# Sixteen attention steps ahead of two MLP layers: one of two heads normalised on ACT, bias tables on GpSimd, one triangle on DVE, and sixty more fill products

## The chip, the core and the metric

The kernel runs on one core of one Trainium2 chip. The core has five engines with queues of their own: TensorE (PE), ScalarE (ACT), VectorE (DVE), GpSimd (POOL) and SyncE (SP), which issues most transfers. The metric is device time in microseconds; less is better. The median of three runs before the change was 915.99 us (913.09 to 917.13).

## What is computed

Attention with a causal window of 128 positions and a linear bias per head, over four sequences of 576 positions with eight heads of 64, then two MLP layers of width 2048 on the 2304 tokens of width 512. The inputs are float32.

```python
def _attn_ref(q, k, v):
    ...
    scores = scale * np.matmul(q, k.transpose(0, 1, 3, 2))
    ...
    bias = slopes[:, None, None] * (-np.abs(rel).astype(np.float32))[None, :, :]
    mask = (rel >= 0) & (rel < window)
    scores = np.where(mask, scores + bias[None], -1000000000.0)
    scores = scores - np.max(scores, axis=-1, keepdims=True)
    attn = np.exp(scores)
    attn = attn / (np.sum(attn, axis=-1, keepdims=True) + 1e-09)
    return np.matmul(attn, v)
...
    h = np.maximum(x @ w_in, 0.0)
    return h * h @ w_out
...
    h = x @ w_in
    g = h * np.cos(h)
    return g @ w_out
```

## The kernel before

Attention is cut into 72 steps. A step is one block of 128 positions (`j`) and one pair of heads: step `a` has `j = a // 4` and heads `2 * (a % 4)` and the next. Blocks whose window lies wholly in the block before and their own are of the kind plain; first, straddle and after are the kinds at the borders of a sequence (`kind`, line 318), and each kind has its own bias table of 128 columns per head in `bias_sb`. `make_bias(0)` makes the tables of the kinds first and plain, `make_bias(1)` those of straddle and after; step 16 (`j` = 4) is the first of the kind straddle.

The first sixteen steps (`START`, line 57) run before any MLP work, two at a time: eight pairs, which are counted from 0 here, pair `k` being steps `2k` and `2k + 1`. For a pair, in this order:

- `scores` (358): TensorE, in float32, into two PSUM banks that pairs use in turn.
- `minima` (403): DVE merges the columns of the block before into those above the diagonal (line 413, not for pairs 0 and 1), then adds the bias and takes the row's extreme, one operation and one read of the accumulator for each of two steps and two heads (line 424).
- `exps` (435): ACT, four exponentials with row sums (line 440).
- `normalise` (449): POOL adds a small number to the four sums (451), DVE takes the reciprocals (452) and multiplies each of the four 128x128 blocks by its own (456).
- `transposes` (458): TensorE turns the four blocks round, ACT copies them out of PSUM (466), and two selects on POOL split them into the part of the own block and that of the block before (469).
- `values` (496): TensorE multiplies with `v`, when the four steps of a block are ready (`values_of_block`). `x_hi` (ACT, 532) and `x_lo` (DVE, 535) then write the two float32r halves of the MLP's input.

Between them stand stages of weight tiles: `w_top` (ACT, 201), `w_rest` (DVE, 205), `w_split` (ACT, 217) and its low part (DVE, 220), with a POOL memset (199). They advance by one stage with each `tick`; new ones start in pairs 3 and 7 only (`START_W`).

The loop at line 739 writes the order out: in round `k` the minima of pair `k + 1`, the exponentials of pair `k`, the values of a block in odd rounds from 3 on, the transposes of pair `k - 1`, the scores of pair `k + 2`, the normalisation of pair `k`. `tc.manual_schedule(engines=ENGINES)` keeps PE, ACT and DVE in that written order; POOL and SP are ordered by a scheduler, and so is everything behind the first MLP unit. Each engine takes its queue strictly in order. After round 7 follow the transposes of pair 7, the values of block 3, and `h_mms(0)` (546), the first hidden unit of the first layer, with its relu on ACT (570). `fill` (112) issues products of a constant bfloat16 tile with itself that nobody reads; 34 of them stand before and between the first scores.

Of the kernel before, what the change touches and what calls it, by code (L numbers as in the profile page):

```python
# [10 lines left out]
BF16 = mybir.dt.bfloat16  # L11
# [4 lines left out]
ALU = mybir.AluOpType  # L16
# [37 lines left out]

START, PLAIN, FILLS = 16, 7, (19, 5, 10)


A_OPEN, START_W = 20, (3, 7)  # L60
# [19 lines left out]
def attention_mlp_mlp(ctx: ExitStack, tc: tile.TileContext, kq, s0, v, w1, w2, bias, ident, out):  # L80
# [262 lines left out]
        k = 512 * (hp // 2) + 256 * what + 128 * (hp % 2)  # L343
        return S0[j][:, k : k + 128]

    def make_bias(part):
        w = slice(256 * part, 256 * part + 256)
        for h in range(H):
            dve.tensor_scalar(bias_sb[:, h, w], base_sb[:, w], 2.0**-h, None, ALU.mult)

    def scores_to(a):
        while now["qk"] < min(a, STEPS - 1):
# [96 lines left out]
    def normalise(*steps):  # L449
        st = St.pop(steps)  # L450
        (pool if len(steps) == 2 else dve).tensor_scalar(st[:, 2], st[:, 1], 1e-9, None, ALU.add)
        dve.reciprocal(st[:, 3], st[:, 2])
        for i, a in enumerate(steps):
            for e in range(2):
                p = Pt[steps][:, 1, i, e]
                dve.tensor_scalar(p, p, st[:, 3, i, e : e + 1], None, ALU.mult)

    def transposes(*steps):

        n = len(steps)  # L460
        pt = Pt.pop(steps)
        tb = ps_s.tile([P, n, 2, P], F32, tag="s", name=f"t_{steps[0]}")
        for i in range(n):
            for e in range(2):
                te.transpose(tb[:, i, e], pt[:, 1, i, e], id_sb)  # L465
        act.copy(pt[:, 0], tb)  # L466
        if kind(steps[0] // 4) != "first":
            for part, sign in ((1, 1), (0, -1)):
                pool.affine_select(  # L469
                    pt[:, part],  # L470
                    pt[:, 0],
                    pattern=[[0, n], [0, 2], [-sign, P]],
                    compare_op=ALU.is_gt if part else ALU.is_ge,
                    fill=0.0,
                    base=0,
                    channel_multiplier=sign,
                )
        for i, a in enumerate(steps):
            Tt[a] = pt[:, :, i]
            waiting.append(a)  # L480

    waiting = []

    def values_of_block():
# [206 lines left out]
    with ExitStack():  # L691
# [12 lines left out]
            above, above, pattern=[[0, 2], [1, P]], compare_op=ALU.is_gt, fill=0.0, base=0, channel_multiplier=-1  # L704
        )
        above = above.bitcast(I32)
        id_sb = kp.tile([P, P], F32, name="id_sb")
        KS = kp.tile([P, 2, H, P], F32R, name="KS")
        base_sb = rp.tile([P, 1024], BF16, tag="a", name="base_sb")
        load_plain(0, slice(0, 1))  # L710
        act.dma_start(base_sb[:, 0:256], bias[:, 0:256])
        make_bias(0)
        load_plain(0, slice(1, 2))
        act.dma_start(id_sb, ident)
        load_plain(1)
# [13 lines left out]


        with tc.manual_schedule(engines=ENGINES):
            pairs = [(s, s + 1) for s in range(0, START, 2)]
            fill(FILLS[0])
            scores(pairs[0])
            fill(FILLS[1])
# [3 lines left out]
            for k in range(len(pairs)):  # L739
                j = k // 2 - 1  # L740
                if k + 1 < len(pairs):
                    minima(pairs[k + 1])
                if k == 0:
                    make_bias(1)
                exps(pairs[k])
                if k % 2 and j >= 0:
                    values_of_block()
                    x_hi(j)
                if k:
                    transposes(*pairs[k - 1])  # L750
                if k + 2 < len(pairs):
                    scores(pairs[k + 2])
                if k + 1 == len(pairs):
                    scores((START,))
                    minima((START,))
                normalise(*pairs[k])
                if k % 2 and j >= 0:
                    x_lo(j)
                tick("aw" if k in START_W else "a")
            transposes(*pairs[-1])  # L760
            for a in pairs[-2]:
                values(a)
            tick("a")
            for k in range(2):
                hps = slice(2 * k, 2 * k + 2)
# [131 lines left out]
```

## Time and profile before

| | |
|---|---|
| median of three runs | 915.99 us (913.09 to 917.13) |
| profiled execution, time | 915.2 us |
| profiled execution, span | 913.5 us |
| mean granted TensorE clock | 0.996 of full speed |
| TensorE busy | 897.2 us, 98% |
| DVE busy | 583.5 us, 64% |
| ACT busy | 470.8 us, 52% |
| POOL busy | 93.6 us, 10% |

Busy shares are means over the whole span. The span is the time from the first to the last instruction; 1.7 us lie around it. The part that the change touches is the first 45 us. A timeline shows instructions in order of time with what ended the wait ahead of them; a chain follows the end back, at each step to what released it; windows give the busy time of each engine in a stretch.

### The profile page before, as it was taken

What the parts mean: (1) busy time and instruction counts of PE and PEld (TensorE: products, weight loads), DVE (VectorE), ACT (ScalarE), POOL (GpSimd) and SP (SyncE); (2) the same over time, 40 slices, a digit from 0 to 9 for tenths busy, and PEclk for the clock granted to TensorE, in tenths of its full rate; (3) what the DMA queues carried; (4) which work ended last, traced back from release to release, by engine and by line L of the source; (5) the groups of instructions that cost most, each with busy time, mean ns of one, the idle gap of its engine ahead of it and who ended that gap; (6) DMA issues with size and microseconds to landing.
All of it is one profiled execution on the core that took longest, in us unless ns stands there. A gap on an engine that the chain in (4) does not pass through costs nothing.

```text
span 913.5 us, 12979 instructions
## 1 busy us (share of the span) xinstructions
PE 897.2 (98%) x4850; PEld 745.6 (82%) x4850; DVE 583.5 (64%) x1351; ACT 470.8 (52%) x1009; POOL 93.6 (10%) x163
## 2 busy tenths in 40 slices
PE   8799999999999999999999999999999999999998
PEld 6577778888888888888888888888888888888897
DVE  7799676666676666745455786665566555655553
ACT  6599554454455444545454774454444444444443
POOL 2333212101111111201011000000000000000000
PEclk9899999999999999999999999999999999999999
DMA  8762131221122111232422530020001000100010
GB/s 343 268 250 58 59 127 59 93 64 64 41 76 81 47 58 47 82 138 93 170 107 98 199 142 1 3 90 1 1 1 47 0 1 1 47 0 1 1 47 24
DMA packets 25870, 69.18 MB, mean 76 GB/s; under 512 B 2640, under 2 KB 8144, under 8 KB 25808
## 3 DMA queue, kind: packets, MB, share of 16 engines
q1 hardware_dynamic: 25376, 68.16, 21.2%
q8 instruction: 38, 0.62, 0.3%
q10 hardware_dynamic: 432, 0.20, 0.1%
q14 instruction: 24, 0.20, 0.1%
HBM read 58.91 MB, written 9.44 MB: 75 GB/s over the span
## 4 chain that ended last, share of the span: by engine, by line
PE 87%; DVE 6%; ACT 4%; issue 1%; DMA 1%; POOL 0%; DVEq 0%; ACTq 0%; POOLq 0%
PE h L564 14%; PE h L565 13%; PE h L566 13%; PE y L641 13%; PE y L643 12%; PE y L642 12%; PE o L512 3%; PE s L374 2%; PE t L465 1%; PE s L394 1%; ACT p L440 1%; PE y L631 1%; PE y L632 1%; PE y L633 1%; DVE s L424 1%
## 5 line engine op out<-in xcount | busy, mean ns | idle before, releaser
L564 PE MATMUL h<-xh,w 128*128 128x512 f32 (+1 forms) x640 | 237.9, 372 | 0.7 <-ACT a L570 0.7
L565 PE MATMUL h<-xl,w 128*128 128x512 f32 (+1 forms) x640 | 236.3, 369 | 0.0
L566 PE MATMUL h<-xh,w 128*128 128x512 f32 (+1 forms) x640 | 236.1, 369 | 0.0
L564 PEld LDWEIGHTS h<-xh,w 128*128 128x128 f32 x640 | 121.0, 189 | 22.1 <-ACT a L570 1.1
L566 PEld LDWEIGHTS h<-xh,w 128*128 128x128 f32 x640 | 120.8, 189 | 20.5
L565 PEld LDWEIGHTS h<-xl,w 128*128 128x128 f32 x640 | 121.1, 189 | 18.9
L641 PE MATMUL y<-rh,w 128*128 128x512 f32 (+1 forms) x320 | 123.4, 385 | 0.5 <-DVE ysb L656 0.5
L643 PE MATMUL y<-rh,w 128*128 128x512 f32 (+1 forms) x320 | 118.5, 370 | 0.0
L642 PE MATMUL y<-rl,w 128*128 128x512 f32 (+1 forms) x320 | 118.4, 370 | 0.0
L594 ACT ACTIVATE r<-r 128x512 f32<-128x512 f32 x72 | 45.5, 632 | 120.3 <-DVE r L593 120.3
L641 PE MATMUL y<-gh,w 128*128 128x512 f32 x256 | 99.6, 390 | 0.2 <-ACT gh L604 0.2
L642 PE MATMUL y<-gl,w 128*128 128x512 f32 x256 | 99.6, 389 | 0.0
L643 PE MATMUL y<-gh,w 128*128 128x512 f32 x256 | 99.6, 389 | 0.0
L605 DVE TENSOR_TENSOR gl<-r,gh 128x512 fp32r<-128x512 f32 x72 | 49.8, 691 | 75.5 <-ACT gh L604 75.5
L591 DVE SCALAR_TENSOR_TENSOR r<-kk,h 128x512 f32<-128x512 int32 x72 | 49.4, 686 | 62.7 <-ACT kk L590 62.6
L581 DVE TENSOR_TENSOR a<-a 128x512 f32<-128x512 f32 x62 | 44.2, 714 | 59.1 <-ACT rh L580 56.3
L590 ACT ACTIVATE kk<-h 128x512 int32<-128x512 f32 x72 | 42.9, 596 | 68.4 <-PE h L566 68.3
L570 ACT ACTIVATE a<-h 128x512 f32<-128x512 f32 x72 | 43.0, 597 | 67.8 <-PE h L566 66.4
L469 POOL TENSOR_SCALAR_AFFINE_SELECT p<-p 128x256 f32<-128x256 f32 x104 | 51.2, 493 | 249.4 <-ACT p L466 245.9
L440 ACT ACTIVATE p<-s,st 128x128 f32<-128x128 f32 x112 | 40.1, 363 | 67.7 <-DVE st L424 63.3
L643 PEld LDWEIGHTS y<-rh,w 128*128 128x128 f32 x320 | 60.3, 188 | 10.6
L641 PEld LDWEIGHTS y<-rh,w 128*128 128x128 f32 x320 | 60.4, 189 | 10.4 <-issue 1.7
(82 smaller groups left out, 1385.0 us busy)
## 6 DMA issues: line engine op xcount, KB each, us to landing
raw<-w_in SPq DMA_DIRECT2D x32, 1023.8 KB, 6.6
raw_a<-kq_in SPq DMA_DIRECT2D x44, 256.0 KB, 2.5
v<-v_in SPq DMA_DIRECT2D x18, 256.0 KB, 2.6
y<-ysb SPq DMA_DIRECT2D x18, 256.0 KB, 2.0
raw_a<-y SPq DMA_DIRECT2D x18, 256.0 KB, 2.7
out<-ysb SPq DMA_DIRECT2D x16, 256.0 KB, 2.4
s<-s_in SPq DMA_DIRECT2D x6, 512.0 KB, 9.4
s<-s_in SPq DMA_DIRECT2D x2, 256.0 KB, 3.6
```

Of the source, the lines that this page charges most:

```text
L440: act.activation(Pt[steps][:, 1, i, e], Sc[a][e][:, own(j)], AF.Exp, bias=st[:, 0, i, e : e + 1], scale=-1.0, accum_out=st[:, 1, i, e : e ...
L469: pool.affine_select(pt[:, part], pt[:, 0], pattern=[[0, n], [0, 2], [-sign, P]], compare_op=ALU.is_gt if part else ALU.is_ge, fill=0.0, b ...
L564: te.matmul(o, wh[:, cs], xh, start=(c == 0 and kt == 0), stop=False, skip_group_check=True)
L565: te.matmul(o, wh[:, cs], xl, start=False, stop=False, skip_group_check=True)
L566: te.matmul(o, wl[:, cs], xh, start=False, stop=(kt == KT - 1), skip_group_check=True)
L581: dve.tensor_tensor(a, a, a, ALU.mult)
L591: dve.scalar_tensor_tensor(r, kk, -C1, hb, ALU.mult, ALU.add)
L594: act.activation(r, r, AF.Abs)
L605: dve.tensor_tensor(rl, r, rh.bitcast(F32), ALU.subtract)
L641: te.matmul(o, wh, gh, start=(first and not (two and m % 2)), stop=False, skip_group_check=True)
L642: te.matmul(o, wh, gl, start=False, stop=False, skip_group_check=True)
L643: te.matmul(o, wl, gh, start=False, stop=last, skip_group_check=True)
```

## The change

Four things. The multiplication by the reciprocal goes to ACT for the second head of each step of a pair. The tables of the kinds straddle and after are made by POOL, behind the normalisation of pair 0. For pair 7 ACT copies the transposed blocks to the place of the part of the block before, where one select on POOL works on them in place, and DVE makes the other part by a multiplication of the PSUM tile with a constant 0/1 triangle, `onward`. And there are more fill products: four ahead of the transposes in rounds 1 to 7, four behind the scores in rounds 0 to 5, and eight between the values of pair 6 and pair 7, 60 in all.

```diff
-START, PLAIN, FILLS = 16, 7, (19, 5, 10)
+START, PLAIN, FILLS = 16, 7, (19, 5, 10, 4, 4, 8)
...
-    def make_bias(part):
+    def make_bias(part, engine):
         w = slice(256 * part, 256 * part + 256)
         for h in range(H):
-            dve.tensor_scalar(bias_sb[:, h, w], base_sb[:, w], 2.0**-h, None, ALU.mult)
+            engine.tensor_scalar(bias_sb[:, h, w], base_sb[:, w], 2.0**-h, None, ALU.mult)
...
                 p = Pt[steps][:, 1, i, e]
-                dve.tensor_scalar(p, p, st[:, 3, i, e : e + 1], None, ALU.mult)
+                r = st[:, 3, i, e : e + 1]
+                if len(steps) == 2 and e:
+                    act.activation(p, p, AF.Copy, scale=r)
+                else:
+                    dve.tensor_scalar(p, p, r, None, ALU.mult)
...
-        act.copy(pt[:, 0], tb)
+        quick = steps == pairs[-1]
+        act.copy(pt[:, 1 if quick else 0], tb)
+        if quick:
+            dve.tensor_tensor(pt[:, 0], tb, onward, ALU.mult)
         if kind(steps[0] // 4) != "first":
-            for part, sign in ((1, 1), (0, -1)):
+            for part, sign in ((1, 1), (0, -1))[: 1 if quick else 2]:
                 pool.affine_select(
                     pt[:, part],
-                    pt[:, 0],
+                    pt[:, part if quick else 0],
...
+        onward = kp.tile([P, 2, 2, P], BF16, name="onward")
+        pool.memset(onward, 1.0)
+        pool.affine_select(
+            onward,
+            onward,
+            pattern=[[0, 2], [0, 2], [1, P]],
...
-        make_bias(0)
+        make_bias(0, dve)
...
-                if k == 0:
-                    make_bias(1)
                 exps(pairs[k])
...
                 if k:
+                    fill(FILLS[3])
                     transposes(*pairs[k - 1])
                 if k + 2 < len(pairs):
                     scores(pairs[k + 2])
+                    fill(FILLS[4])
...
                 normalise(*pairs[k])
+                if k == 0:
+                    make_bias(1, pool)
...
             for a in pairs[-2]:
                 values(a)
+            fill(FILLS[5])
```

In the rows that follow, `st` tiles hold the sums and reciprocals of one pair, `s_0`, `s_1` with three figures are the banks of scores, `s_0_110` to `s_6_116` the tiles in which the exponentials of a pair stand, `t` the transposed pair in PSUM. Lines 458 and 471 of the changed kernel are the normalisation on ACT and the copy.

POOL, from the constants to the add of pair 2, before:

```order
L703 AFFINE_SELECT above<-above 128x256
L451 TENSOR_SCALAR st_224<-st_224 128x4
L451 TENSOR_SCALAR st_229<-st_229 128x4
L199 MEMSET cv_w_1_550 128x1024
L451 TENSOR_SCALAR st_264<-st_264 128x4
```

and now:

```order
L717 AFFINE_SELECT onward<-onward 128x512
L451 TENSOR_SCALAR st_227<-st_227 128x4
L349 TENSOR_SCALAR bias_sb<-base_sb 128x256 x8
L199 MEMSET cv_w_0_405 128x1024
L451 TENSOR_SCALAR st_232<-st_232 128x4
L199 MEMSET cv_w_1_605 128x1024
L451 TENSOR_SCALAR st_271<-st_271 128x4
```

The eight bias operations and the memset of the first weight tile, which stood ahead of the constants' select, now stand between the adds of pair 0 and pair 1.

ACT, from the last exponential of pair 0 to the first of pair 2, before:

```order
L440 ACTIVATE s_0_110,st_224<-s_1_198,st_224 128x128
L440 ACTIVATE s_1_111,st_229<-s_0_208,st_229 128x128
L440 ACTIVATE s_1_111,st_229<-s_1_209,st_229 128x128
L440 ACTIVATE s_1_111,st_229<-s_0_208,st_229 128x128
L440 ACTIVATE s_1_111,st_229<-s_1_209,st_229 128x128
L466 COPY s_0_110<-t_273 128x512
L440 ACTIVATE s_2_112,st_264<-s_0_246,st_264 128x128
```

and now:

```order
L440 ACTIVATE s_0_110,st_227<-s_1_201,st_227 128x128
L458 ACTIVATE s_0_110<-s_0_110,st_227 128x128 x2
L440 ACTIVATE s_1_111,st_232<-s_0_211,st_232 128x128
L440 ACTIVATE s_1_111,st_232<-s_1_212,st_232 128x128
L440 ACTIVATE s_1_111,st_232<-s_0_211,st_232 128x128
L440 ACTIVATE s_1_111,st_232<-s_1_212,st_232 128x128
L471 COPY s_0_110<-t_284 128x512
L458 ACTIVATE s_1_111<-s_1_111,st_232 128x128 x2
L440 ACTIVATE s_2_112,st_271<-s_0_241,st_271 128x128
```

The normalisations of a pair stand between its exponentials and those of the next pair, behind the copy of the pair before it.

ACT at the end of the sixteen steps, from the high half of x in round 7 to the copy of pair 7, before:

```order
L440 ACTIVATE s_0_110,st_476<-s_1_453,st_476 128x128
L532 CAST xh_106<-o_503 128x4x128
L466 COPY s_6_116<-t_523 128x512
L201 CAST cv_w_1_550<-raw_1_169 128x1024
L466 COPY s_0_110<-t_553 128x512
```

and now:

```order
L440 ACTIVATE s_0_110,st_523<-s_1_496,st_523 128x128
L540 CAST xh_106<-o_554 128x4x128
L471 COPY s_6_116<-t_578 128x512
L458 ACTIVATE s_0_110<-s_0_110,st_523 128x128 x2
L201 CAST cv_w_1_605<-raw_1_172 128x1024
L471 COPY s_0_110<-t_608 128x512
```

The cast of the second weight tile stands behind the normalisation of pair 7 and ahead of the copy that waits for its transposes.

## Rows read from the trace of the kernel before

**Rows 1.** Page: busy time, and the granted clock in 40 equal slices.

```profile
PE 897.2 (98%) x4850; PEld 745.6 (82%) x4850; DVE 583.5 (64%) x1351; ACT 470.8 (52%) x1009; POOL 93.6 (10%) x163
...
PEclk9899999999999999999999999999999999999999
```

**Rows 2.** Stretches: length, busy (instructions) of PE, PEld, DVE, ACT, POOL, granted clock, DMA.

```profile
25.00:30.00 5.00, 2.32 (x30) 1.82 (x30) 4.89 (x24) 2.66 (x11) 3.34 (x6) 1.00 1.03 402
...
20.00:40.00 20.00, 15.51 (x158) 12.58 (x160) 15.09 (x63) 11.03 (x36) 9.45 (x15) 0.88 0.72 270
40.00:60.00 20.00, 19.31 (x94) 14.54 (x91) 17.04 (x44) 18.03 (x35) 5.86 (x8) 0.95 0.79 300
60.00:80.00 20.00, 19.20 (x118) 14.52 (x117) 18.15 (x37) 19.10 (x38) 6.36 (x9) 1.00 0.23 82
```

**Rows 3.** Stretches of one microsecond around the gap of TensorE, same columns.

```profile
32.00:33.00 1.00, 0.07 (x2) 0.00 (x0) 0.90 (x7) 1.00 (x2) 0.59 (x1) 1.00 1.08 301
...
35.00:36.00 1.00, 1.00 (x9) 0.80 (x10) 1.00 (x2) 0.58 (x1) 0.20 (x1) 0.68 1.00 401
36.00:37.00 1.00, 1.00 (x12) 1.00 (x10) 0.15 (x1) 0.00 (x0) 0.93 (x2) 0.50 1.10 467
```

**Rows 4.** Chain that ended last, first 60 us: start, us, what.

```profile
8.16 1.03 DVE bias_sb L349 x8
...
12.82 0.87 DVE s L456 x4
13.70 0.67 DVE s L413 x2
...
15.51 0.87 DVE s L456 x4
...
33.24 0.60 DVE s L456
```

**Rows 5.** Timeline, 7 to 24 us: start, us, engine, line, operation [idle before].

```profile
6.96 1.27 PE L114 MATMUL junk<-idle 128*128 128x256 bf16 x10
...
8.24 0.31 POOL L451 TENSOR_SCALAR st<-st 128x4 f32<-128x4 f32 x1 [5.55 <-ACT s L440]
...
12.47 0.37 ACT L440 ACTIVATE s<-s,st 128x128 f32<-128x128 f32 x1 [0.43 <-DVE st L424]
...
14.06 0.22 POOL L451 TENSOR_SCALAR st<-st 128x4 f32<-128x4 f32 x1 [3.11 <-ACT s L440]
...
20.06 0.64 ACT L466 COPY s<-t 128x512 f32<-128x512 f32 x1
...
23.38 0.58 ACT L532 CAST xh<-o 128x512 fp32r<-128x512 f32 x1 [0.25 <-PE o L512]
```

**Rows 6.** Timeline: value products early and late, and the first relu.

```profile
15.11 1.09 PE L512 MATMUL o<-s,v 128*64 128x128 f32 x16
...
35.49 1.98 PE L512 MATMUL o<-s,v 128*64 128x128 f32 x16
...
38.55 1.97 PE L512 MATMUL o<-s,v 128*64 128x128 f32 x16
...
44.32 0.60 ACT L570 ACTIVATE a<-h 128x512 f32<-128x512 f32 x1 [0.46 <-PE h L566]
```

**Rows 7.** Durations by line, first 45 us: ns, least/median/most; starts; shapes.

```profile
L199 POOL MEMSET cv_w<- x4: 952/953/955, 1.3 to 43.2; 128x1024 f32 x4
...
L703 POOL TENSOR_SCALAR_AFFINE_SELECT above<-above x1: 407/407/407, 2.3 to 2.3; 128x256 f32<-128x256 f32 x1
...
L469 POOL TENSOR_SCALAR_AFFINE_SELECT s<-s x12: 637/637/1147, 17.7 to 36.7; 128x512 f32<-128x512 f32 x12
...
L201 ACT CAST cv_w<-raw x3: 1380/1381/1381, 17.5 to 42.5; 128x1024 f16<-128x1024 bf16 x3
...
L217 ACT CAST w<-cv_w x2: 1047/1048/1048, 24.4 to 40.8; 128x1024 fp32r<-128x1024 f32 x2
...
L220 DVE TENSOR_TENSOR w<-cv_w,w x2: 1209/1217/1225, 27.1 to 41.9; 128x1024 fp32r<-128x1024 f32 x2
```

More of the change, by code (lines that the diff above doesn't have):

```diff
@@ L480, in transposes @@
             waiting.append(a)
+    pairs = [(s, s + 1) for s in range(0, START, 2)]
     waiting = []
@@ L706, in attention_mlp_mlp @@
         above = above.bitcast(I32)
+        onward = kp.tile([P, 2, 2, P], BF16, name="onward")
[4 more added lines that the diff above has]
+            pattern=[[0, 2], [0, 2], [1, P]],
+            compare_op=ALU.is_ge,
+            fill=0.0,
+            base=0,
+            channel_multiplier=-1,
+        )
         id_sb = kp.tile([P, P], F32, name="id_sb")
@@ L731, in attention_mlp_mlp @@
         with tc.manual_schedule(engines=ENGINES):
-            pairs = [(s, s + 1) for s in range(0, START, 2)]
             fill(FILLS[0])
```

## The prediction

> **What bounds the kernel now.** I read the page's busy table first. TensorE is busy 98% of the span at a granted clock of 0.9 or more of full speed in every slice of the clock row but the second [rows 1]. The stretches of 20 us come next: from 20 to 40 us TensorE is busy 15.51 us of 20 and the clock is 0.88, in the two stretches after that it is busy over 19 us [rows 2]. All that the change touches ends at about 44 us, where the relu of the first hidden unit starts [rows 6]. So the question is by how much that relu, and the ACT work around it, comes earlier or later. Whatever it is, it runs through to the end: ACT is busy 18.03 and 19.10 us of the two stretches that follow, mostly with splitting weights [rows 2], and cannot make up lateness there; behind that TensorE sets the pace, as its 98% of the whole span says [rows 1].
>
> Next the chain that ended last, for the first 45 us. From 8 to 26 us it stays on DVE: bias tables 1.03, then for each pair the merge (0.67), four minima and four normalisations (0.87), 2.69 from one pair to the next [rows 4]. The normalisations begin at 12.82 for pair 1 and at 33.24 for pair 7 (I count pairs from 0), 20.4 us for six pairs, with two waits of the split of a weight tile and three low halves of x in between.
>
> Last, TensorE by the microsecond: it is busy 0.07 us in the microsecond from 32 to 33, while it waits for the normalisation of pair 7; from 35 to 36 the granted clock is 0.68, in the next microsecond 0.50, which is 1.2 of 2.4 GHz [rows 3]. Behind that sixteen value products take 1.97 us, earlier 1.09 [rows 6].
>
> **Bias tables on GpSimd.** DVE loses eight operations, 1.03 us of its chain [rows 4]. They go to POOL's queue, and there the order puts all eight, and a memset of a weight tile (0.95, [rows 7]) that used to run before 3 us, between the add of pair 0 and the add of pair 1. The reciprocal of pair 1 waits for that add, and behind it on DVE wait all further minima, on ACT the new normalisations. No row has a POOL tensor_scalar of 128x256 in bfloat16. Bounds: the four-element add, 0.22 [rows 5], and the select of 128x512, 0.64 without interference; nearest is the select of 128x256, 0.407 [rows 7], and I take 0.41. The add of pair 0 ends at 8.55 [rows 5]; 8.55 + 8 x 0.41 + 0.95 + 0.22 is 13.0, and with 0.3 for the reciprocal normalisation 1 starts at 13.3, 0.5 later than now. With 0.22 the queue no longer decides: DVE is ready for pair 1 at about 11.5. With 0.64 it is 15.1. Behind 16 us nobody waits for these tables: the kinds that they serve start with step 16.
>
> The Trainium skill, GPSIMD Engine Reference, section 3.1, gives 1.03 cycles of 1.2 GHz per element for operations with little work in them. As an estimate from that page, 256 elements are 0.22 us on top of what a tiny operation takes, 0.44 in all, and the sum below would end 0.2 us later. No run here shows it yet.
>
> **Half of the normalisations on ACT.** DVE loses two of four per pair, 0.43 of 0.87 [rows 4]. ACT gains two, of a form that no row has; the exponential of the same shape takes 0.37, and four of them with the reads of their accumulators, which the new operation does not have, 1.5 [rows 5]. I take 0.30, between DVE's 0.22 and 0.37. Now the order matters more than the sum. Before, ACT ran the exponentials of pair k+1 while DVE normalised pair k. In the new order ACT's two normalisations of pair k stand between the two, and they wait for POOL's add and DVE's reciprocal, which wait for the exponentials of pair k. So ACT gets a loop of its own: from the first exponential at 12.47 to the add at 14.06 are 1.6 us, the add takes 0.22 [rows 5], the reciprocal and its hand-over about 0.3, so 2.1, and the copy of a transposed pair (0.6) fits between; then two normalisations, 0.6: 2.7 us. In pairs 3, 5 and 7 the high half of x stands there too and makes it 3.1. Pairs 2 to 7: 3 x 2.7 + 3 x 3.1 = 17.4; the two weight casts on ACT, 1.38 and 1.05 long, of which some 0.1 overlaps with the next operation [rows 7], make it 19.9. That is 0.5 less than the 20.4 of now, if nothing else waits.
>
> But ACT's copy of the transposed pair, the selects and the value products now sit in this loop too. Carried forward queue by queue with the same durations, three waits come out. In pair 5 the high half of x waits for values whose selects start only after exponentials 4; copy, selects and values took 3.3 us (20.06 to 23.38), ACT gets there after 2.7, and the next copy waits for four fill products and the transposes behind the values: 1.4 together. In pair 6 the weight cast (1.05) now follows normalisation 5, DVE's subtraction (1.21) waits for it, minima 7 (1.67) wait for that, and the reciprocal comes 1.1 after ACT wants it. In pair 7 the chain copy, selects, values, fill, transposes, scores and minima of step 16 is 5.9 us against 4.6 on ACT, 1.2. Sum 3.7; I take 23.3 us for the six pairs, since part of the cast is counted in the wait of pair 6, and 36.6 for normalisation 7, 3.4 later than now; with no waits it is 33.2, as now.
>
> The Trainium skill speaks against this step: ScalarE: Activation LUTs, Rules for kernel authors, leaves multiplications to VectorE. As an estimate from its formula (section What ACT_TABLE_LOAD costs) one such operation is 386 ns, 93 of it overlapped, so 0.29 us; the row of the exponential, 367 ns, agrees to 0.02. By the rule alone ACT pays 0.6 where DVE saves 0.43, and the sum stays as it is.
>
> **The last pair and the order at the end.** One select instead of two before the value products saves 0.64; DVE's triangle runs beside ACT's copy and costs nothing, but the weight cast of 1.38 on ACT now stands between normalisation 7 and that copy, as the rows of ACT's order show, and takes some 0.6 back. The scores of step 17, which now stand ahead of the last values (these start at 38.55, [rows 6]), move partly behind them. From normalisation 7 to the relu are now 11.1 us (33.24 to 44.32). With the clock held: cast and copy to 2.5, select 0.7, second half of the values 0.7, twelve hidden products of 0.23 and their end 3.3, with the waits between them 7.5: 3.6 less. At half clock the values, the scores and the first hidden products are 2.6 longer, as they are now.
>
> **Fill products.** Sixty are added, 0.107 to 0.127 us each at full clock (ten took 1.27, [rows 5]), 7 us in all. Those behind the scores are covered by TensorE's waits for DVE or ACT. Four before the transposes cost up to 0.43 where the values came last (counted above). None stands between the scores of step 16 and the transposes of pair 7, which is where TensorE idles before the clock falls. Whether 0.43 before that gap and 0.86 behind it hold the clock is the open question. I expect that they just do, since the stretch from 25 to 30 us of now, with 2.32 busy us of 5, still had 1.00 [rows 2].
>
> **The sum.** Normalisation 7 3.4 later, the tail 3.6 shorter: 0.2 us earlier at the relu. On the profiled execution that is 915.2 - 0.2 = 915.0; the median of the three runs lies 0.8 above it, so **915.8 us**. Some later loads move in SP's queue; I cost them at nothing, as ACT stays busy over 90% from 40 to 80 us [rows 2]; if that cover failed, a load would show as a wait on ACT there.
>
> **Rivals.** *The clock falls all the same.* The gap that no fill covers is about as long as now. Then the tail is only 1.0 shorter, the net is 2.4 later, and the time 918.4. Against it: the products in front of the gap are denser.
>
> *ACT is no bound.* If the three waits vanish because the queues settle otherwise, and the bias operations take 0.22 to 0.41, normalisation 7 comes at 33.2 to 31.4, up to 1.8 earlier, and with the shorter tail the whole 3.6 to 5.4: 910.6 to 912.4. For it speaks that DVE, now the chain, loses 4.5 us; against it that the loop through ACT, POOL and DVE leaves 0.5 us at best.
>
> *POOL's queue holds up pair 1.* Place: the add of pair 1 behind eight bias operations and the memset. Each tenth of a microsecond per operation costs 0.8. From 0.44 on the kernel is slower than before with the clock held. At 0.64 it is 1.6 slower, 917.6; with the clock fallen too 4.2, 920.2. Slower by over 0.5%, 4.6 us (about what a measurement of this kernel can tell from no change), needs 1.0 per operation with the clock held or 0.7 with it fallen.
>
> **How the numbers follow.** Forecast 0.42, clock 0.26, no bound 0.22, POOL 0.10. Faster by over 0.5% is below 911.4: some two thirds of the second rival, 0.14. Slower is above 920.6: most of the last, 0.09. The rest, 0.77, is no measurable change. The range reaches from the best end of the second rival, 910.6, to 920.0; outside lie most of the last rival, 0.09, and what of the second would gain still more, 0.08.
>
> **What the profile after would show.** Right: POOL starts the add of pair 1 near 12.8; ACT waits for DVE's reciprocal before its normalisations; normalisation 7 after 35 us; the value products of pair 7 near 0.95 us and a clock of 1.00 from 30 to 45. Wrong: bias operations far from 0.41, exponentials that follow one another without those waits, a slice at 0.50, or a relu of the first unit away from 44 by more than 3 us.

## The result, and the profile after

The changed kernel is slower: 926.07 us (median of 4 runs, 925.45 to 926.26) against 915.41 of the kernel before beside it, a ratio of 1.0117 (95% interval 1.0093 to 1.0141). The prediction was 915.8, between 910.6 and 920.0. The profiled execution has a span of 924.1 us, 10.6 more than before, and the relu of the first hidden unit starts at 55.44 instead of 44.32 [rows 6], 11.1 later. So all of the loss arises in the first 55 us, as the prediction had placed it, and almost nothing of it is made up.

Page of the changed kernel: busy times, and the granted clock in 40 slices.

```profile
PE 905.9 (98%) x4910; PEld 752.5 (81%) x4910; DVE 581.1 (63%) x1328; ACT 475.5 (51%) x1025; POOL 98.9 (11%) x172
...
PEclk8999999999999999999999999999999999999999
```

Beside [rows 1] this shows nothing: the shares are the same, and a slice of 23 us is too coarse for the clock. Stretches of the same trace (columns as in [rows 2]):

```profile
10.00:15.00 5.00, 3.88 (x42) 3.04 (x38) 2.06 (x11) 2.28 (x11) 4.81 (x7) 1.00 1.03 430
15.00:20.00 5.00, 1.34 (x6) 1.01 (x7) 2.34 (x12) 2.17 (x11) 3.33 (x6) 0.70 1.00 415
20.00:25.00 5.00, 5.00 (x42) 4.04 (x42) 3.19 (x20) 2.99 (x12) 0.44 (x2) 0.62 0.83 343
...
40.00:45.00 5.00, 4.05 (x32) 3.04 (x32) 1.10 (x8) 2.65 (x11) 1.50 (x3) 0.66 0.56 197
45.00:50.00 5.00, 4.35 (x31) 3.15 (x32) 3.35 (x9) 2.73 (x5) 0.64 (x1) 0.77 0.67 280
...
60.00:80.00 20.00, 19.26 (x100) 14.59 (x99) 19.27 (x48) 19.11 (x38) 8.22 (x11) 1.00 0.58 220
```

From 10 to 15 us POOL, the engine with the least work, is busy 4.81 of 5, while DVE and ACT do 2.06 and 2.28 us of work and TensorE stops at 13.88. The granted clock falls twice: at 15 to 25 us, and again from 40 us on. From 60 to 80 us ACT is busy 19.11 of 20, about as in [rows 2], so there is no idle time in which lateness could be made up. The chain that ended last (start, us, what) says what POOL does; in [rows 4] it stood on DVE there:

```profile
7.48 1.52 ACT s L440 x8
9.07 0.23 POOL st L451
9.38 3.30 POOL bias_sb L349 x4
12.74 0.85 POOL bias_sb L349
...
16.32 0.89 POOL cv_w L199
17.29 0.24 POOL st L451
17.55 0.19 DVE st L452
17.84 0.78 DVE s L460
```

The eight table operations take 6.94 us, 0.87 from one to the next, then comes the memset, and only at 17.29 the add of pair 1. Before, it stood here:

```profile
9.63 0.31 POOL L451 TENSOR_SCALAR st<-st 128x4 f32<-128x4 f32 x1 [1.08 <-ACT s L440]
```

The timeline of the changed kernel shows who waited for it (in brackets the idle time and what ended it), and a second queue on POOL later:

```profile
17.55 0.18 DVE L452 RECIPROCAL st<-st 128x4 f32<-128x4 f32 x1 [5.50 <-POOL st L451]
...
17.83 0.69 ACT L458 ACTIVATE s<-s,st 128x128 f32<-128x128 f32 x2 [5.53 <-DVE st L452]
...
18.66 1.12 PE L469 MATMUL t<-id_sb,s 128*128 128x128 f32 x4 [4.78 <-DVE s L460]
...
37.35 0.95 POOL L199 MEMSET cv_w<- 128x1024 f32 x1 [1.43 <-DVE w L220]
...
39.96 1.11 PE L520 MATMUL o<-s,v 128*64 128x128 f32 x16 [2.54 <-POOL s L476]
...
55.44 0.60 ACT L578 ACTIVATE a<-h 128x512 f32<-128x512 f32 x1 [0.25 <-PE h L574]
```

DVE, ACT and TensorE stand still for some five microseconds each. At 37 us a memset of a weight tile, which waits for DVE, stands in POOL's queue ahead of the two selects that the value products need. The first starts at 38.25, 0.33 behind the end of its copy; the add of pair 6 comes next, and the second starts at 39.27. TensorE is idle for 2.54 us, and the second fall of the clock follows that gap.

### The profile page after: what moved, and what is told of

It is laid out like the page before. It is cut to its first block, busy times and chain, and to the rows that moved or that the text cites. A ratio compares the mean times of both kernels' runs of the same rounds, so it can differ in the third digit from the quotient of the medians.

```text
span 924.1 us, 13111 instructions
## 1 busy us (share of the span) xinstructions
PE 905.9 (98%) x4910; PEld 752.5 (81%) x4910; DVE 581.1 (63%) x1328; ACT 475.5 (51%) x1025; POOL 98.9 (11%) x172
## 4 chain that ended last, share of the span: by engine, by line
PE 89%; DVE 5%; ACT 3%; POOL 1%; issue 1%; DMA 1%; DVEq 0%; ACTq 0%; POOLq 0%; SPq 0%
PE h L572 14%; PE h L573 13%; PE h L574 13%; PE y L649 13%; PE y L651 12%; PE y L650 12%; PE o L520 3%; PE s L374 2%; PE t L469 2%; PE s L394 1%; DVE w L220 1%; PE junk L114 1%; DVE cv_w L205 1%; PE y L640 1%; PE y L639 1%
## 5 line engine op out<-in xcount | busy, mean ns | idle before, releaser
L572 PEld LDWEIGHTS h<-xh,w 128*128 128x128 f32 x640 | 120.7, 189 | 21.2 <-ACT a L578 0.5
L574 PEld LDWEIGHTS h<-xh,w 128*128 128x128 f32 x640 | 120.7, 189 | 20.4
L651 PEld LDWEIGHTS y<-rh,w 128*128 128x128 f32 x320 | 60.3, 189 | 10.7
```

Of the source, the lines that this page charges most:

```text
L572: te.matmul(o, wh[:, cs], xh, start=(c == 0 and kt == 0), stop=False, skip_group_check=True)
L574: te.matmul(o, wl[:, cs], xh, start=False, stop=(kt == KT - 1), skip_group_check=True)
L651: te.matmul(o, wl, gh, start=False, stop=last, skip_group_check=True)
```

## The experiments

One row for each kernel but the probe of prices: start of normalisation 1 and 7, the time between them (pairs 2 to 7), start of the first relu, all from its profiled execution; the median, and its ratio to the kernel before beside it with the 95% interval. Executions differ in when the first scores' inputs land (the products of pair 1 start at 6.31 before and at 7.26 after), so normalisation 1 moves by up to 0.9 without any change.

| kernel | norm. 1 | pairs 2-7 | norm. 7 | relu | median us | ratio |
|---|---|---|---|---|---|---|
| before | 12.82 | 20.4 | 33.24 | 44.32 | 915.41 | |
| changed | 17.84 | 27.4 | 45.22 | 55.44 | 926.07 | 1.0117 (1.0093 to 1.0141) |
| e1_tables_dve | 13.63 | 25.3 | 38.94 | 50.40 | 919.66 | 1.0055 (1.0037 to 1.0073) |
| e13_tables_dve_pinned | 13.98 | 23.7 | 37.64 | 47.97 | 918.16 | 1.0039 (1.0024 to 1.0054) |
| e14_quick_fills_pinned | 12.96 | 22.1 | 35.09 | 43.28 | 915.66 | 1.0003 (0.9991 to 1.0016) |
| e3_tables_norm_dve | 13.64 | 25.2 | 38.83 | 48.57 | 918.89 | 1.0040 (1.0025 to 1.0055) |
| e2_only_tables_pool | 16.96 | 23.2 | 40.11 | 52.69 | 923.14 | 1.0089 (1.0063 to 1.0115) |
| e5_only_fills | 13.40 | 25.3 | 38.65 | 48.37 | 918.98 | 1.0039 (1.0024 to 1.0054) |
| e9_fills_memset_pinned | 13.65 | 22.1 | 35.78 | 45.54 | 915.78 | 1.0008 (0.9996 to 1.0020) |
| e8_fills_pool_by_hand | 11.87 | 29.3 | 41.18 | 52.75 | 923.05 | 1.0082 (1.0065 to 1.0098) |
| e7_only_norm_act | 12.92 | 25.6 | 38.50 | 50.80 | 922.08 | 1.0071 (1.0050 to 1.0091) |
| e16_norm_act_pinned | 13.50 | 25.9 | 39.43 | 51.89 | 922.67 | 1.0090 (1.0073 to 1.0107) |
| e15_norm_act_behind | 12.30 | 23.8 | 36.09 | 48.42 | 920.32 | 1.0061 (1.0046 to 1.0076) |
| e6_only_quick | 12.65 | 20.4 | 33.08 | 42.72 | 913.64 | 0.9977 (0.9967 to 0.9987) |
| e4_fill_gap | 13.06 | 20.4 | 33.48 | 41.91 | 912.45 | 0.9978 (0.9965 to 0.9991) |
| e11_quick_gap | 13.01 | 20.4 | 33.43 | 41.62 | 912.33 | 0.9976 (0.9966 to 0.9985) |
| e12_tables_late | 12.35 | 21.2 | 33.56 | 41.45 | 911.88 | 0.9969 (0.9958 to 0.9979) |

### The price of a table operation

> The kernel before with 24 operations on GpSimd and 4 on ACT, on tiles that nobody else uses, added behind the last select: a look at prices alone. If bfloat16 makes the table operation dear: 128x256 in bfloat16 near 0.85 us as in the changed kernel, the same multiplication in float32 near 0.41 like the select of 128x256. If the multiplication by a scalar does it: both near 0.85, and the plain copy in bfloat16 below 0.5. If the start of an operation does it: 128x128 costs as much as 128x256; if the elements do, half. A Copy with a scale on ACT, 128x256: 0.45.

```diff
+        with tc.issue_after(now["sel"].ins):
...
+            for _ in range(6):
+                pool.tensor_scalar(bo[:, 0:256], bf[:, 0:256], 0.5, None, ALU.mult)
+                pool.tensor_scalar(bo[:, 0:128], bf[:, 0:128], 0.5, None, ALU.mult)
+                pool.tensor_scalar(fo[:, 0:256], ff[:, 0:256], 0.5, None, ALU.mult)
+                pool.tensor_copy(bo[:, 0:256], bf[:, 0:256])
+            for _ in range(4):
+                act.activation(ab[:, 0:256], bf[:, 0:256], AF.Copy, scale=0.5)
```

Its instructions by tile (ns: least/median/most):

```profile
L845 POOL TENSOR_SCALAR pr_bo<-pr_bf x6: 845/849/1172, 392.0 to 406.8; 128x256 bf16<-128x256 bf16 x6
L846 POOL TENSOR_SCALAR pr_bo<-pr_bf x6: 526/528/1536, 393.6 to 408.1; 128x128 bf16<-128x128 bf16 x6
L848 POOL COPY pr_bo<-pr_bf x6: 393/396/497, 395.4 to 409.7; 128x256 bf16<-128x256 bf16 x6
...
L847 POOL TENSOR_SCALAR pr_fo<-pr_ff x6: 846/847/1177, 392.8 to 399.9; 128x256 f32<-128x256 f32 x6
...
L850 ACT ACTIVATE pr_ab<-pr_bf x4: 411/416/418, 391.6 to 394.0; 128x256 bf16<-128x256 bf16 x4
```

It is the multiplication, not the type: 0.85 in bfloat16 and in float32. 128 elements more cost 0.32 us, 2.5 ns each, and a copy of the same block takes 0.40, which is what the select takes [rows 7] and what the prediction had taken for the table operation. ACT would need 0.42.

### Taking the change back, part by part

> The changed kernel with the tables of straddle and after made by DVE again, at the place that they had before; the rest of the change stays. Theory A (the price of the table operations on GpSimd, 0.87 us each, holds the add of pair 1 up to 17.29, TensorE idles 4.8 us, its clock falls, and most of the loss comes from there): normalisation 1 near 12.8, the six pairs to normalisation 7 in 23.3 us instead of 27.4, the first relu at 43.6 if the clock holds and at 46.3 if it falls in the gap before the last values; 914.7 or 917.4 us. Rival B (the loop of ACT, POOL and DVE that the normalisations on ACT make is the cause by itself): the six pairs still take 27.4, the relu comes at 50.4, 921.5 us.

Against the changed kernel:

```diff
+                if k == 0:
+                    make_bias(1, dve)
                 exps(pairs[k])
...
-                if k == 0:
-                    make_bias(1, pool)
```

50.40, 919.66: the tables on POOL cost 5.0 us at the relu. Both theories were half right: the wait at pair 1 went (13.63), but the six pairs still took 25.3, and the relu came where rival B had put it. And here POOL's memsets, which now run beside the tables on DVE, make these slow:

```profile
8.02 2.72 DVE L349 TENSOR_SCALAR bias_sb<-base_sb 128x256 bf16<-128x256 bf16 x8
...
8.61 1.99 POOL L199 MEMSET cv_w<- 128x1024 f32 x2
```

2.72 us for the eight, against 1.17 in the kernel before, where no memset runs beside them; with one memset beside them, in e7, they take 1.95.

> As e1_tables_dve (the changed kernel with its tables on DVE), and the memset of the third weight tile tied behind the last select before it, so that it stands behind the selects of pair 7. If the loop through ACT costs by itself: the memset is worth at most the 1.0 us by which the second select of pair 5 was late, normalisation 7 at 37.5 to 38.9, relu 48.5 to 50.4, 918 to 919.7 us. If most of the waits of that loop came from the memset, as with the fills alone: relu 45.5 to 47, 916 us.

The edit, here and in every kernel called pinned:

```diff
-                pool.affine_select(
+                now["sel"] = pool.affine_select(
...
-        pool.memset(job.t, 0.0)
+        with ExitStack() as x:
+            if job.key[1:] == (0, 2):
+                x.enter_context(tc.issue_after(now["sel"].ins))
+            pool.memset(job.t, 0.0)
```

23.7 for the six pairs, relu 47.97, 918.16: the time lies in the range for the loop alone, the relu 0.5 below it and 1 above that for the memset alone. The pin, which also puts the add of pair 6 back ahead of the selects, was worth 2.4 at the relu; the loop remains. Little of the 2.4 is the wait itself: TensorE's gap ahead of the values of pair 5 shrinks from 2.54 to 1.97 us only, but the clock stays at 1.00 behind it until 39 us, where in e1 it fell at 35. The waits of ACT in pairs 5, 6 and 7, with the clock held so far, are the best view of the loop:

```profile
27.32 0.59 ACT L543 CAST xh<-o 128x512 fp32r<-128x512 f32 x1 [0.99 <-PE o L523]
...
28.30 0.59 ACT L474 COPY s<-t 128x512 f32<-128x512 f32 x1 [0.38 <-PE t L472]
...
33.47 0.69 ACT L461 ACTIVATE s<-s,st 128x128 f32<-128x128 f32 x2 [1.18 <-DVE st L455]
...
37.63 0.70 ACT L461 ACTIVATE s<-s,st 128x128 f32<-128x128 f32 x2 [1.12 <-DVE st L455]
```

> As e3_tables_norm_dve (the quick last pair and the sixty fills), with the memset tied in the same way. It is e9_fills_memset_pinned plus the quick last pair, which gained 1.6 us at the relu by itself: relu 44.0, 914.2 us. Against e13_tables_dve_pinned it gives the price of the normalisations on ACT with everything else mended: 4.5 to 6.4 us at the relu if the loop is the cause, under 3 if not.

```diff
-                if len(steps) == 2 and e:
+                if False and e:
```

That edit (no normalisation on ACT) on top of e13 brings the relu to 43.28, 4.7 us earlier, within what was expected for the loop. But only 1.5 of the 4.7 arise in the six pairs (23.7 against 22.1). Another 1.0 is there at normalisation 1 already, where the tables of e13 run beside memsets (2.71 us) and those of e14 don't (1.17). The last 2.1 arise behind normalisation 7, where the clock falls in e13 (0.70 from 40 to 45 us) and holds in the execution shown of e14. That execution took 913.6. Of the ten, four took 913.6 to 913.9 with a mean granted clock of 1.000, and six 915.7 to 917.3 with 0.995 to 0.998, so the 4.7 belongs to the better four. By the medians, each less that of the kernel before beside it, the excess goes from 10.7 (changed) to 5.6 (e1), 3.1 (e13) and 0.6 (e14): 5.1 for the tables, 2.5 for the memset, 2.5 for the normalisations, taken back in this order.

### Each part alone

> The kernel before with one thing of the change: the tables of straddle and after made by GpSimd behind the normalisation of pair 0. Theory A: eight operations of 0.87 put the add of pair 1 at 15.5 (here no memset stands between), normalisation 1 at 15.9, 3.1 later than before; the chain of DVE runs on as before, 2.7 per pair, so the relu is at 47.4 or later where the clock falls; 918.3 us or more. Rival B: DVE, which loses 1.03 us of work, catches up, the relu within 1 us of 44.3; 914 to 916 us.

From here on the edits are against the kernel before, where nothing else is said.

```diff
-                if k == 0:
-                    make_bias(1)
...
                 normalise(*pairs[k])
+                if k == 0:
+                    make_bias(1, pool)
```

```profile
9.36 6.97 POOL L349 TENSOR_SCALAR bias_sb<-base_sb 128x256 bf16<-128x256 bf16 x8
...
16.41 0.23 POOL L451 TENSOR_SCALAR st<-st 128x4 f32<-128x4 f32 x1
...
16.67 0.18 DVE L452 RECIPROCAL st<-st 128x4 f32<-128x4 f32 x1 [4.30 <-POOL st L451]
```

DVE loses 1.03 us of work and gains a wait of 4.30. The relu is 8.4 late, 923.14: more than the 4.1 at normalisation 1 (of which 0.8 are inputs that landed later); the clock is 0.50 from 15 to 20 us and 0.59 to 25, and again below 0.65 from 40 to 50 us. Theory A stands and was too low.

> The kernel before with one thing of the change: the quick last pair with its triangle on DVE. In GpSimd's order the memset of the third weight tile stands behind the selects of pair 5, as before. Normalisation 7 within 0.4 us of 33.24, the tail to the relu 0.6 shorter: relu 43.7, 914.6 us. If the cast that stands ahead of the last copy, or the lower clock, eats the 0.6: relu 44.3, 915.2 us.

```diff
-        act.copy(pt[:, 0], tb)
+        quick = steps == pairs[-1]
+        act.copy(pt[:, 1 if quick else 0], tb)
+        if quick:
+            dve.tensor_tensor(pt[:, 0], tb, onward, ALU.mult)
```

Relu 42.72, 913.64, faster by 0.23%: 1.6 at the relu instead of the 0.6 expected. The two halves of the values now follow each other, 3.35 us for both, and the scores of step 17 come behind them (39.24 instead of 37.40).

> The kernel before with one thing of the change: the second head of each step normalised on ACT. If the loop of ACT, POOL and DVE is what the change adds by itself: pairs 2 to 7 in 25.3 us, as with the tables on DVE in the changed kernel (e1_tables_dve), instead of 20.4, relu 48.5 to 49.5, 918 to 920 us. If the waits in that loop were made by the fills alone: 20.4 to 21.5 us, relu under 46, 917 us at most.

```diff
-                dve.tensor_scalar(p, p, st[:, 3, i, e : e + 1], None, ALU.mult)
+                r = st[:, 3, i, e : e + 1]
+                if len(steps) == 2 and e:
+                    act.activation(p, p, AF.Copy, scale=r)
+                else:
+                    dve.tensor_scalar(p, p, r, None, ALU.mult)
```

25.6 for the six pairs, as the loop gives; the relu, 50.80, and the time, 922.08, are later than the 48.5 to 49.5 and 918 to 920 expected, with the clock at 0.50 from 35 to 45 us. ACT's wait before its normalisations of pairs 6 and 7:

```profile
32.69 0.69 ACT L458 ACTIVATE s<-s,st 128x128 f32<-128x128 f32 x2 [1.59 <-DVE st L452]
...
38.48 0.69 ACT L458 ACTIVATE s<-s,st 128x128 f32<-128x128 f32 x2 [1.69 <-DVE st L452]
```

> The kernel before with one thing of the change: the sixty fill products. Theory C (the fills change the order that the scheduler gives GpSimd: the memset of the third weight tile now stands ahead of the add of pair 6 and the selects of pair 5, and it waits for DVE's low half of the first weight tile): the selects of pair 5 start 1.5 to 2 us after the copy that they read, as in e3_tables_norm_dve (29.86 to 31.91), the values of pair 5 follow as late, the clock falls there, normalisation 7 at 36 to 38, relu 47 to 48, 917 to 918 us. Rival D (what costs is TensorE's time for four fills in front of the transposes): no such wait on GpSimd, up to 0.43 in each of three pairs, relu below 45.7, under 916.5 us.

```diff
-START, PLAIN, FILLS = 16, 7, (19, 5, 10)
+START, PLAIN, FILLS = 16, 7, (19, 5, 10, 4, 4, 8)
...
+                    fill(FILLS[3])
                     transposes(*pairs[k - 1])
...
+                    fill(FILLS[4])
...
+            fill(FILLS[5])
```

```profile
29.03 0.61 ACT L466 COPY s<-t 128x512 f32<-128x512 f32 x1
29.08 1.21 DVE L220 TENSOR_TENSOR w<-cv_w,w 128x1024 fp32r<-128x1024 f32 x1
...
30.35 0.95 POOL L199 MEMSET cv_w<- 128x1024 f32 x1 [2.06 <-DVE w L220]
...
31.68 1.41 POOL L469 TENSOR_SCALAR_AFFINE_SELECT s<-s 128x512 f32<-128x512 f32 x2
...
33.14 1.94 PE L512 MATMUL o<-s,v 128*64 128x128 f32 x16 [2.79 <-POOL s L469]
```

Products that nobody reads, on an engine that waits anyway, cost 3.3 us (918.98 against 915.66; 917 to 918 was expected), by the way of another engine's queue: the copy is done at 29.64, the selects start at 31.68 behind a memset that waited for DVE, and TensorE idles 2.79 us, after which the sixteen products take 1.94 instead of 1.09. Whether theory C or D, the next run tells. The fills are not the only edit that moves the memset: in e7, without a fill, it starts at 30.53, the two selects of pair 5 at 31.44 and 32.46 behind it, with the add of pair 6 between them as in the changed kernel. In e2 and e6 it stands behind the selects.

> The sixty fills, as in e5_only_fills, with one tie: the memset of the third weight tile is issued behind the last select that stands before it in the code, so it follows the selects of pair 7, and the rest of GpSimd's order is that of the kernel before. Theory C (the loss of the fills comes from that memset, which waits for DVE in front of the selects of pair 5): the selects of pair 5 start within 0.3 us of the end of their copy instead of 2.0, normalisation 7 at 33.5 to 35, relu at 44 to 46 instead of 48.37, 915 to 917 us. Rival D (TensorE's time for the fills): the time of e5_only_fills, 919 us, within 0.7.

```profile
29.27 0.61 ACT L469 COPY s<-t 128x512 f32<-128x512 f32 x1
...
29.49 0.93 POOL L454 TENSOR_SCALAR st<-st 128x4 f32<-128x4 f32 x1 [0.96 <-ACT s L443]
...
30.49 1.34 POOL L472 TENSOR_SCALAR_AFFINE_SELECT s<-s 128x512 f32<-128x512 f32 x2
...
31.89 1.09 PE L515 MATMUL o<-s,v 128*64 128x128 f32 x16 [1.49 <-POOL s L472]
```

The pin of e13 on top of e5. The selects start 0.6 behind the copy, not 2.0 (0.3 was expected; the add of pair 6 ahead of them took 0.93 instead of 0.22). Relu 45.54, 915.78, with normalisation 7 at 35.78, a little above the 33.5 to 35 of theory C: that theory holds for 2.8 of the 4.1 us at the relu. Without that memset the fills cost nothing that can be told from no change in the time (1.0008, 0.9996 to 1.0020), but the trace still shows something: the six pairs take 22.1 instead of 20.4 and the relu is 1.2 later than before. That fits rival D, TensorE's time for the fills ahead of the transposes.

> The changed kernel with the tables and all the normalisations back on DVE: what is left is the quick last pair and the sixty fill products. Theory A and B alike: normalisation 7 within 0.5 us of the 33.2 of before, the tail 0.6 shorter by the select; relu 43.7, 914.6 us. If the fills also hold the clock behind pair 7: 2.6 less, 41.1, 912.0 us. If the fills stand in the way of the values: up to 0.43 for each of three pairs, 916 us.

e14 without the pin. 48.57, 918.89, a miss: I had not yet seen the memset. Its selects of pair 5 start at 31.91, two microseconds behind their copy, as in e5; with the memset tied, e14, the same edits stand at 43.28.

> The sixty fills, as in e5_only_fills, but GpSimd's queue in the written order too, which puts the memset of the third weight tile behind the selects of pair 7. Theory C: the selects follow their copies at once, normalisation 7 at 33.3 to 34.5, relu within 1 us of 44.3, 914 to 916 us. Rival D: the same time as e5_only_fills within 0.5 us.

```diff
-ENGINES = {mybir.EngineType.PE, mybir.EngineType.Activation, mybir.EngineType.DVE}
+ENGINES = {mybir.EngineType.PE, mybir.EngineType.Activation, mybir.EngineType.DVE, mybir.EngineType.Pool}
```

```profile
17.47 1.35 POOL L469 TENSOR_SCALAR_AFFINE_SELECT s<-s 128x512 f32<-128x512 f32 x2 [4.14 <-ACT s L466]
18.90 0.22 POOL L451 TENSOR_SCALAR st<-st 128x4 f32<-128x4 f32 x1
...
19.16 0.18 DVE L452 RECIPROCAL st<-st 128x4 f32<-128x4 f32 x1 [2.05 <-POOL st L451]
```

923.05: no test of C, since the written order puts the add of a pair behind the selects of the pair before, and the chain of DVE through them. It shows the same sensitivity from the other side: against e9 the order on the least busy engine is worth 7 us at the relu.

### Loop or work on ACT

> As e7_only_norm_act with the memset tied behind the selects, to be set against e15_norm_act_behind. Loop as the cause: normalisation 7 at 37.5 to 38.5, relu 49 to 50.8, 918 to 922 us. Memset as the cause: normalisation 7 under 36, relu under 48, under 918 us.

e7 with the pin: 25.9, 51.89, 922.67, no earlier than without it. That the memset costs nothing here is not shown, though: behind the same two gaps of TensorE, 1.14 and 0.71 us, which end by 12.0 us there and 12.6 here, the clock is 1.00 from 15 to 20 us in e7 and 0.53 here, and what the pin gains can lie under that fall.

> As e7_only_norm_act, with ACT's two normalisations of a pair issued behind the exponentials of the next pair, as ACT has time for them then, and the memset tied behind the selects. If it is the order that costs (the exponentials of the next pair wait for the reciprocal): the waits of ACT for DVE's reciprocal go, pairs 2 to 7 in 21 to 23.5 us instead of 25.6, relu 46 to 48.5 instead of 50.8, 916 to 918.5 us. If it is ACT's time or the lateness of the transposes: 25 us or more, relu 50 or later.

```diff
                 if len(steps) == 2 and e:
-                    act.activation(p, p, AF.Copy, scale=r)
+                    behind.append((p, r))
...
                 exps(pairs[k])
+                normalise_act()
```

Against e16 the six pairs take 23.8 instead of 25.9 and the relu comes 3.5 earlier, but 920.32 is above the range given for the order. The 2.1 us are not the order alone: e15 is at full clock from 10 to 20 us, where e16 is at 0.79 and 0.53. Over pairs 2 and 3, where e7 is at full clock too, the order gains 0.3 (5.14 against 5.39). In e15 other waits stand in place of ACT's for the reciprocal: the transposes wait for ACT's normalisations, 2.23 us at 20.99 and 1.97 at 29.15. So the lateness of the transposes is a part of the rest; how large it is, no run separates.

### Versions that gain

> The kernel before with twelve fill products, 1.5 us at full clock, ahead of the transposes of pair 7, where TensorE waits from 32.07 to 33.89 for the normalisation. If the idle gap there is what lowers the clock at 35.35: no slice at half clock, both runs of value products 1.09 instead of 1.97, the relu 2.6 earlier, 912.8 us. If the clock falls all the same: 915.4 us, or up to 0.3 more where the last fill is late.

```diff
+            fill(12)
             transposes(*pairs[-1])
```

Before, with a stretch of five microseconds as the last line (columns as in [rows 2]):

```profile
33.89 0.33 PE L465 MATMUL t<-id_sb,s 128*128 128x128 f32 x1 [1.81 <-DVE s L456]
...
35.00:40.00 5.00, 5.00 (x37) 4.25 (x38) 1.57 (x3) 0.96 (x2) 1.49 (x2) 0.54 0.68 282
```

and now:

```profile
32.24 1.48 PE L114 MATMUL junk<-idle 128*128 128x256 bf16 x12
...
34.13 0.33 PE L465 MATMUL t<-id_sb,s 128*128 128x128 f32 x1 [0.40 <-DVE s L456]
...
35.69 1.09 PE L512 MATMUL o<-s,v 128*64 128x128 f32 x16
...
35.00:40.00 5.00, 4.78 (x47) 3.74 (x46) 2.23 (x4) 2.18 (x4) 1.48 (x2) 1.00 0.84 317
```

The idle gap shrinks from 1.81 to 0.40 us, the clock is 1.00 from 35 to 40 us where it was 0.54, and the products take 1.09 instead of 1.98 [rows 6]: 912.45. Twelve fills at the one gap ahead of the fall do what sixty elsewhere did not.

> The kernel before with the quick last pair of the change and with twelve fill products ahead of the transposes of pair 7, and nothing else. If the two gains add: no slice at half clock from 30 to 45 us, the 32 last value products in 2.0 us instead of 3.35, relu 41.1, 911.5 to 912.5 us. If they are the same gain twice: 912.5 to 913.6, the better of the two alone.

The edits of e6 and e4 together. Relu 41.62, 912.33: the gains do not add. The time lies in the range given for gains that add, but e4 alone has 912.45, and the ratios are 0.9976 and 0.9978. With the clock held the quick pair is worth 0.3 at the relu.

> As e11_quick_gap, with the tables of straddle and after split: the first two heads on DVE as before (0.26 us in its chain instead of 1.03), the other six on GpSimd behind the last select of pair 7, where it is idle until the next weight tile. If only the place of the tables was wrong in the changed kernel: normalisation 1 at 12.0, everything behind it 0.77 earlier, relu 40.3, 0.8 us less than e11_quick_gap. If GpSimd's six operations of 0.87 slow DVE or come too late for step 17 or hold up the load that waits for their input: the same or up to 2 us more.

Against e11:

```diff
-                    make_bias(1, dve)
+                    make_bias(1, dve, range(2))
...
             transposes(*pairs[-1])
+            with tc.issue_after(now["sel"].ins):
+                make_bias(1, pool, range(2, H))
```

Pairs 1 to 5 start 0.7 earlier than in e11, and then, in the execution shown, the clock falls at another place:

```profile
20.00:25.00 5.00, 5.00 (x52) 4.44 (x50) 4.89 (x26) 2.21 (x10) 2.13 (x4) 0.66 0.38 156
```

Its 32 value products there take 3.07 us instead of 1.97, and the lead is gone at pair 7: relu 41.45, not the 40.3 expected. This execution took 912.93; eight of the eleven have a mean granted clock of 0.999 or more, against its 0.998, and take 910.9 to 912.1. The median, 911.88, is the lowest of all, but its interval overlaps with those of e11 and e4.

## Why the prediction was wrong, point by point

- **What bounds the kernel, and where the change acts: right.** All of the difference is made before the first relu (11.1 us there, 10.6 at the end).
- **The price of the table operation: the first step that failed.** The prediction took 0.41, nearest row the select, and 0.64 as upper bound; it is 0.85, above the bound. A select bounded a multiplication because it was the nearest in shape; it was not the nearest in kind. The term, eight operations, was 3.3 us and measured 6.94; the add of pair 1 started at 17.29 instead of 12.8, and 0.8 of that is that the first inputs landed later in this execution. The rival "POOL's queue holds up pair 1" had the place and the waiting engines right, with a chance of 0.10. At 0.85 its formula gives 915.8 + 8 x 0.44, 919.3, and with the clock fallen 921.9; the 926.07 lie above both, in part because a second step failed too (POOL's order, below). Taking the tables back gave 5.1 of the 10.7 us (e1). The estimate from the Trainium skill, GPSIMD Engine Reference, section 3.1, 0.44 by 1.03 cycles per element, was no better; the same section has 2.6 for operations with two inputs, and names VectorE as the rule for elementwise work. Here the trace shows 2.5 ns per element, which is 3.0 cycles of 1.2 GHz, and decides.
- **The clock: the rival was right, and too small.** It expected one fall, at 35 us; there are two. The first is behind the wait for POOL, with 0.70 and 0.62 from 15 to 25 us, where scores and values are slow. There ACT's normalisation of pair 3 comes 5.4 after that of pair 2 (20.52 to 25.95); at full clock, in e1, it is 3.7. The eight fills that follow the scores of round 1 end at 13.88, and the wait of 4.78 comes behind them.
- **The loop on ACT: right where it was not disturbed, and not by luck.** The prediction said 23.3 for pairs 2 to 7; e13 shows 23.7, with two normalisations in 0.69 and the pair without extras at 2.69 (13.98 to 16.67), expected 2.7. The three waits that it added, 1.4, 1.1 and 1.2 in pairs 5, 6 and 7, are 1.37, 1.18 and 1.12 there. (Its own terms without waits, 17.4 and the two casts, make 19.8 and not 19.9.) In the changed kernel it is 27.4: 1.6 more by the memset (e1 less e13), and 2.1 more than e1, likely by the first fall of the clock, though no run separates it.
- **The tail: right for the rival, too short for the forecast.** From normalisation 7 to the relu the forecast took 7.5 us with the clock held, 3.6 less than before; where it holds (e14) it is 8.2. With the clock fallen the rival had 10.1, and the changed kernel shows 10.2.
- **POOL's order behind pair 2, and the fills: the second step that failed.** The fills were costed as time on TensorE, at most 0.43 a pair. That was near: 1.3 for the three pairs in which it was counted, and with the memset tied the six pairs take 1.7 more (e9). The order of POOL was read up to the add of pair 2 and taken as unchanged behind it, a term put at nothing. There a memset that waits for DVE came to stand ahead of the selects of pair 5, through the scheduler that orders POOL: 2.5 us of the 10.7 (e13), and 2.8 of the 4.1 at the relu that the fills cost alone (e9). The fills move it by themselves (e5), and so do the normalisations on ACT (e7); which of the two does it in the changed kernel stays open. The order of POOL in pairs 5 and 6 could have been read ahead of the run.
- **The quick last pair: right in sign**, 1.6 alone and 0.3 with the clock held.
- **The parts do not add.** Alone the tables cost 8.4 at the relu, the normalisations 6.5 and the fills 4.1, the quick pair gains 1.6: 17.4, against 11.1 together. A reading that fits, but that no run tests: while one queue is stalled the other waits lie under it, and a clock that has fallen does not fall again. The memset ahead of the selects also stands in two of these kernels, e5 and e7.

## What to carry to other kernels

An idle engine is a cheap place for work only if nothing urgent stands behind it in its queue: ask what its next small operation releases, and price the moved operation by a row of the same operation, or measure it, before its share is called free. After any edit read again the order of every engine that a scheduler fills, also those that the edit doesn't touch, and look there for an instruction that waits ahead of one that others wait for. Fill products paid here in the gap just ahead of a fall of the clock, which one trace showed; and where executions of one kernel differ in the clock, a single profile is one of two cases.

## What the runs showed of the hardware

- GpSimd multiplies 128x256 by a scalar in 0.85 us, in bfloat16 and in float32 alike, and copies it in 0.40; DVE makes the same eight tables in 1.17 (0.22 for one, overlapping).
- DVE and GpSimd hold each other up. Eight tables on DVE took 2.72 us beside two memsets on GpSimd (e1), one of them 1.07 instead of 0.22. In e12 six multiplications on GpSimd took 7.77 us beside DVE's weight splits, the slowest 1.89 instead of 0.85. In e9 an add of four columns on GpSimd took 0.93 instead of 0.22 beside DVE's split (1.21). The Trainium skill, SBUF — State Buffer, Who interferes with whom, describes an exclusive lock on a port that the two share; the operation of 1.07 us beside a memset of 0.95 agrees with that.
- The granted clock fell behind gaps of TensorE of 4.78, 2.54 and 2.79 us (changed, e5), and held behind one of 0.40 (e4). In the kernel before it fell behind one of 1.81, and in e9, behind gaps of 1.49 and 1.53, the value products of pair 7 took 1.97; in e14 it held behind 1.48 and 1.53, and in e13 behind 1.97. Behind the same two gaps, 1.14 and 0.71, it held in e7 and fell in e16. So the length of a gap alone did not tell whether the clock falls.
